# A planner's order in place of a scheduler's, in a kernel of linear attention and a feed-forward layer

## The chip, the cores and the metric

The kernel runs on one core of one Trainium2 chip. The metric is the device time of one execution in microseconds; the median of several executions counts, and lower is better.

## What is computed

The reference has two parts. The first is an attention without softmax that carries a state: for each of 4 batches and 8 heads, over 768 steps, with vectors of 48 numbers,

```
y[t]  = r[t] (state + (u * k[t]) v[t]^T)
state = w * state + k[t] v[t]^T
```

where `w` is a decay per head and channel (0.85 to 0.95 in the inputs) and `u` a bonus. The results of all heads form x, 3072 tokens of 384 numbers. The second part is a feed-forward layer:

```
h = x @ w_in          # 384 -> 2048
g = h - tanh(h)
out = g @ w_out       # 2048 -> 384
```

`r`, `k`, `v`, `w`, `u` come as float32. The two weights come as float64 (6.29 MB each); the kernel reads their 64-bit words as integers and makes float32 of them on the chip.

## The kernel before

**Units.** The attention part is cut into 24 units. A unit is 64 steps (`SHORT`) of two batches, all 8 heads. Unit n belongs to chunk n // 2, and the two units of a chunk cover the four batches. The function `near` is for decays near one (0.5 to 2); a flag, computed on the chip, says whether they are, and the function `anywhere` takes over if not. In this profile `near` alone does work.

**The steps of a unit** (`unit`, lines 385 to 470). Six DMAs of 96 KB bring r, k and v in two halves each. TensorE transposes r (`turn`, L402) into `x_ps`; VectorE multiplies it by the powers of the decay (`rT`, L411). k is multiplied by the inverse powers (`kw`, L413), transposed and copied by ACT (`kT`, L415). A product r*k*u, summed per head, gives `du` (L409, L417, L418), which becomes a diagonal `at` (L420, eight ACT instructions). TensorE multiplies the state by rT (L431), then kT by rT (the levels, L435). VectorE writes the levels into `at` where a mask says so (L437, the mask step). TensorE forms the outputs from v and `at` (L442) and the state's addition from kw and v (L449). ACT copies the outputs to `xt` and `rest` (L451, L456); after every second unit, POOL issues six small DMAs that fill the rest of `xt` (L460, the fills). VectorE adds to the state (L466), POOL multiplies it by the decay (L469). The first 16 units are "early": their r*k, u and kw products run on VectorE; in the later ones these and the diagonal run on POOL.

**Tiles.** Two units make a block of 256 tokens; there are 12. The 2048 hidden features are done 256 at a time; one block and 256 features is a tile, so there are 96. A tile has an h part (L156, 6 matmuls of 256 columns, in two halves, into one of two PSUM buffers), five ACT operations (L167 to L171: s, th, tg, q, small), four VectorE operations (L172 to L175: g, two products on tg, and a copy where x is small), and an o part (L184, 4 matmuls of 384 columns). Every matmul in float32 is two instructions in the profile. The o part of a tile is put two tiles behind its h part (the list `waiting`).

**Weights.** There are 16 pieces of 768 KB (`Weights`): two of w_in, two of w_out, in turn. A piece of w_in comes in four DMAs, one of w_out in one. Four staging buffers hold pieces. Converting a piece takes five VectorE and two ACT instructions (L130 to L140). In the kernel before, all pieces are loaded by POOL's queue, the next one into a buffer when its conversion is written out.

**What sets the order.** The first six blocks (`FIRST`) go through the features in four quarters: quarter 0 of blocks 0 to 5, then quarter 1, and so on, so that only a quarter of the weights is needed at first. Partial sums are kept (`part`) and added (L192). Blocks 6 to 11 take all features at once. Beside the tiles of blocks 0 to 5, the functions `weave` and `steady` mix the units of the blocks ahead and the conversions in proportion to their numbers of steps. The start up to unit 1 and pieces 0 and 1 is written out by hand (`go`), through the class `Written`, which keeps the order as written; its line in the profile is L230 for all operations. Behind that, the framework's own scheduler orders each engine's instructions from its own costs.

Of the kernel before, what the change touches and what calls it, by code (L numbers as in the profile page):

```python
# [2 lines left out]

# [6 lines left out]
F32 = mybir.dt.float32  # L10
U32 = mybir.dt.uint32
I32 = mybir.dt.int32
# [65 lines left out]
class Weights:  # L78
# [28 lines left out]
    def load(self, n, queue=None):  # L107
        if n >= self.count:
            return
        dst, parts = self.piece(n)  # L110
        if self.sources[n % 4 > 1].dtype == I64:
            self.staged[n] = st = self.stage.tile([128, self.COLS], I64, name="st", tag="st", bufs=4)
            dst = st.rearrange("p (k f) -> p k f", k=dst.shape[1])
        for to, src in parts:
            (queue or self.nc.sync).dma_start(out=dst[to], in_=src)  # L115

    def convert(self, n, V=None, A=None):


        if n not in self.staged:  # L120
            return
        V, A = V or self.nc.vector, A or self.nc.scalar
        dst = self.piece(n)[0].rearrange("p k f -> p (k f)")
        st = self.staged.pop(n)
        words = st.bitcast(U32).rearrange("p (n t) -> p n t", t=2)
        lo, hi = words[:, :, 0], words[:, :, 1]
        lo_f = st.bitcast(F32).rearrange("p (n t) -> p n t", t=2)[:, :, 0]
        power = self.stage.tile([128, self.COLS], U32, name="power", tag="power", bufs=2)
        bits = dst.bitcast(U32)
        V.tensor_scalar(power, hi, 0x7FF00000, None, ALU.bitwise_and)  # L130
        V.tensor_scalar(bits, hi, 0xFFFFF, 0x100000, ALU.bitwise_and, ALU.bitwise_or)
        yield
        A.activation(power, power, AF.Relu, scale=8.0, bias=self.bias)
        A.activation(lo_f, lo, AF.Copy, scale=2.0**-52)
        yield
        V.scalar_tensor_tensor(dst, bits, 2.0**-20, lo_f, ALU.mult, ALU.add)
        yield
        V.scalar_tensor_tensor(power, hi, 0x80000000, power, ALU.bitwise_and, ALU.bitwise_or)  # L138
        yield
        V.tensor_tensor(dst, dst, power.bitcast(F32), ALU.mult)  # L140
        yield


def make_dense(nc, work, gpool, ps_d, shared, out, rows):

    V, A, T = nc.vector, nc.scalar, nc.tensor
    d, w_in_sb, w_out_sb = (shared[x] for x in ("dims", "w_in", "w_out"))
    m1b, smallb = (shared[x] for x in ("m1b", "smallb"))

    waiting, sums = [], {}  # L150

    def first(xt, f):
        h = ps_d.tile([128, 2, d.NT], F32, name="h", tag="h")
        for z in range(2):
            for kk in range(d.NK):
                T.matmul(h[:, z], w_in_sb[:, f // 2, kk, z * 128 : (z + 1) * 128],  # L156
                         xt[:, kk].rearrange("p b t -> p (b t)"),
                         start=kk == 0, stop=kk == d.NK - 1)
        hf = h.rearrange("p z t -> p (z t)")

        def tmp(name):
            return work.tile([128, 2 * d.NT], F32, name=name, tag=name)

        s, th, tg, q, small = (tmp(x) for x in ("s", "th", "tg", "q", "small"))
        g = gpool.tile([128, 2, d.NT], F32, name="g", tag="g")
        gf = g.rearrange("p z t -> p (z t)")
        A.activation(s, hf, AF.Square)  # L167
        A.activation(th, hf, AF.Tanh)  # L168
        A.activation(tg, hf, AF.Tanh, scale=G1)  # L169
        A.activation(q, s, AF.Square, bias=m1b)  # L170
        A.activation(small, s, AF.Relu, bias=smallb, scale=-1.0)  # L171
        V.tensor_tensor(gf, hf, th, ALU.subtract)  # L172
        V.scalar_tensor_tensor(tg, s, C4, tg, ALU.mult, ALU.mult)  # L173
        V.scalar_tensor_tensor(tg, q, K1, tg, ALU.add, ALU.mult)  # L174
        V.copy_predicated(gf, small.bitcast(I32), tg)  # L175
        return g

    def second(j, fs, f, g):
        if f == fs[0]:
            sums["now"] = [ps_d.tile([128, d.DM], F32, name=f"o{i}", tag=f"o{i}", bufs=1) for i in range(L)]  # L180
        outs = sums["now"]
        for z in range(2):
            for i in range(L):
                T.matmul(outs[i], g[:, z, i * C : (i + 1) * C], w_out_sb[:, f + z, :],  # L184
                         start=f + z == fs[0], stop=f + z == fs[1] - 1)
        if f + 2 < fs[1]:
            return
        begun, whole = fs[0] > 0, fs[1] == d.NF
        for i in range(L):
            if begun:  # L190
                o = sums.pop((j, i)) if whole else sums[j, i]
                V.tensor_tensor(o, outs[i], o, ALU.add)  # L192
            else:
                if whole:
                    o = work.tile([128, d.DM], F32, name="o", tag="o")
                else:
                    o = sums[j, i] = work.tile([128, d.DM], F32, name="part", tag="part", bufs=L * FIRST)
                A.copy(o, outs[i])  # L198
            if whole:
                runs = rows(L * j + i)  # L200
                n = C // len(runs)
                for z, row in enumerate(runs):
                    nc.sync.dma_start(out=out[row : row + n, :], in_=o[z * n : (z + 1) * n])

    def dense(j, xt, fs=(0, d.NF)):

        for f in range(fs[0], fs[1], 2):
            waiting.append((j, fs, f, first(xt, f)))
            if len(waiting) > 2:
                second(*waiting.pop(0))  # L210
            yield

    def finish():
        while waiting:
            second(*waiting.pop(0))

    return dense, finish


class Written:  # L220


    def __init__(self, tc, engine):
        self.tc, self.engine, self.last = tc, engine, None

    def __getattr__(self, name):
        op = getattr(self.engine, name)

        def issue(*args, **how):
            self.last = self.tc.keep_in_program_order(op(*args, **how))  # L230
            return self.last

        return issue


def steady(d, first, unit, dense, finish, nstep, new_xt, xts):
# [5 lines left out]
    for j in range(0 if first else 2):  # L242
        weave(blocks(j))
    for j in range(first, d.NB):
        streams = [(dense(j, xts.pop(j)), d.NF // 2)]
# [7 lines left out]
def near(ctx, tc, r, k, v, w, u, out, shared, weights):  # L253
# [3 lines left out]
    V, A, T, G = nc.vector, nc.scalar, nc.tensor, nc.gpsimd  # L257
# [13 lines left out]

    engines = {x: Written(tc, getattr(nc, x)) for x in ("vector", "scalar", "tensor", "sync")}
    V, A, T, Q = engines.values()
    A.activation(fixed("warm", [128, 1]), shared["one"], AF.Tanh)
    ps = ps_a.tile([128, 2, 512], F32, name="x_ps", tag="x_ps")
    rows = fixed("rows", [NP, 2, PAD])
    V.memset(rows, 1.0)  # L280
    Q.dma_start(out=rows[:, :, :D], in_=w.rearrange("(p i) d -> p i d", i=2))
# [6 lines left out]
    ub = fixed("ub", [128, H, D])  # L288
# [10 lines left out]
    HALF = [slice(z * SHORT, (z + 1) * SHORT) for z in range(2)]  # L299
    loaded = {}  # L300

    def fetch(n, parts="rkv", queue=None):
        ch, half = divmod(n, 2)
        at = slice(ch * SHORT, (ch + 1) * SHORT)
        if n not in loaded:
            kt = load.tile([128, H, D], F32, name="kt", tag="kt")
            loaded[n] = {"r": rts[n % (AHEAD + 1)], "k": kt, "v": vts[n % (AHEAD + 1)]}
        for x in parts:
            src = {"r": r, "k": k, "v": v}[x]
            for z in range(2):  # L310
                (queue or Q).dma_start(out=loaded[n][x][HALF[z], :, :D],
                                       in_=src[half * 2 + z, :, at, :].rearrange("h t d -> t h d"))

    fetch(0, "r")
    fetch(0, "k", A)
    weights.load(0, G)
    Q.dma_start(out=ub.rearrange("p h d -> p (h d)"),
                in_=bass.AP(tensor=u.tensor, offset=u.offset, ap=[[0, 128], [1, H * D]]))
    fetch(1, "rk")
    weights.load(1, G)  # L320
    fetch(0, "v")
    fetch(1, "v")
    weights.load(2, G)
    weights.load(3, G)
    fetch(2)

    wcol = ps[:, 1, :NP]
    T.transpose(wcol, rows.rearrange("p i d -> p (i d)"), ident[:NP, :NP])  # L330
    power = fixed("power", [128, NP, SHORT + 1])
    inverse = fixed("inverse", [128, NP, SHORT + 1])
    V.tensor_scalar(by[:, :, 1:], wcol[:, :, None].to_broadcast([128, NP, SHORT]), W_LOW, W_HIGH, ALU.max, ALU.min)
    flat = "d p n -> d (p n)"
    V.tensor_tensor_scan(power.rearrange(flat), by.rearrange(flat), plus.rearrange(flat), 0.0, ALU.mult, ALU.add)
    V.reciprocal(inverse, power)

# [474 lines left out]
```

## Time and profile before

| | us |
|---|---|
| Median of 3 executions (655.8 to 656.92) | 656.14 |
| The profiled execution | 655.85 |
| Its span in the profile | 654.1 |
| TensorE matmuls busy | 604.0 |
| VectorE busy | 419.2 |
| ScalarE busy | 365.2 |
| GpSimd busy | 134.7 |

The profile is one execution, with times counted from the start of its span; what lies around the span is 1.75 us. PE is TensorE, DVE VectorE, ACT ScalarE, POOL GpSimd, SP the engine that issues most DMAs. "L383" is line 383 of the kernel. "Idle before" is the time that an engine stood before an instruction, and the name after the arrow is what ended it. DMA share is the mean busy share of the core's 16 DMA engines.

### The profile page before, as it was taken

The page shows a single profiled execution, that of the slowest core. Times are in us where ns is not written, and L with a number is a line of the kernel's source. Part 1 is how long each engine was busy: PE and PEld are TensorE (multiplying, and loading weights), DVE is VectorE, ACT ScalarE, POOL GpSimd, SP SyncE. Part 2 cuts the span into 40 slices and gives each one's busy share as a digit, 9 for nine tenths or more (in the row PEclk, how much of TensorE's full clock was granted, in tenths as well). Part 3 has the DMA queues.
Part 4 walks back from the last instruction along what each step waited for, and adds up shares of the span by engine and source line. Part 5 has one row for each costly group of instructions (what it writes and reads, how often), then busy time and mean ns, then how long its engine had stood idle before and what let it go on. Part 6 is the DMA issues. An engine that isn't in the chain of part 4 may idle for free.

```text
span 654.1 us, 12775 instructions
## 1 busy us (share of the span) xinstructions
PE 604.0 (92%) x5063; PEld 445.8 (68%) x5063; DVE 419.2 (64%) x659; ACT 365.2 (56%) x740; POOL 134.7 (21%) x185
## 2 busy tenths in 40 slices
PE   2358998999999999999999999999999999999994
PEld 1346765676777777777777777777777777777772
DVE  4578998999856566656665755646645544555551
ACT  3356876877665554555555554554554554655552
POOL 5142452546001121104000132332321201000000
PEclk9999999999999999999999999999999999999998
DMA  9897674871010100101011120220110000100001
GB/s 153 196 158 177 105 134 135 138 172 37 8 25 13 27 18 6 33 1 31 25 25 48 43 56 13 42 51 9 33 29 2 15 17 5 29 1 2 24 1 29
DMA packets 85857, 33.76 MB, mean 52 GB/s; under 512 B 78620, under 2 KB 82972, under 8 KB 85788
## 3 DMA queue, kind: packets, MB, share of 16 engines
q1 hardware_dynamic: 78972, 18.89, 15.9%
q0 software_dynamic: 5760, 13.77, 8.8%
q8 instruction: 42, 0.69, 0.4%
q10 hardware_dynamic: 1056, 0.20, 0.2%
q14 instruction: 27, 0.22, 0.1%
HBM read 26.94 MB, written 4.72 MB: 48 GB/s over the span
## 4 chain that ended last, share of the span: by engine, by line
PE 79%; DVE 8%; DMA 5%; issue 3%; ACT 2%; POOL 1%; SPq 1%; DVEq 0%; POOLq 0%
PE h L156 36%; PE o L184 35%; PE yk_ps L383 5%; DMA kt<-in_k_dram 2%; PE x_ps L402 2%; DMA st<-in_moe_w_out_dram 2%; PE x_ps L383 1%; DMA rt<-in_r_dram 1%; POOL xt L460 1%; SPq L230 1%; DVE g L172 1%; DVE power L138 1%; DVE at L437 0%; DVE tg L173 0%; DVE du L418 0%
## 5 line engine op out<-in xcount | busy, mean ns | idle before, releaser
L156 PE MATMUL h<-xt,w_in_sb 128*128 128x256 f32 x1152 | 273.0, 385 | 7.9 <-DMA xt<-rest 7.9
L184 PE MATMUL o<-w_out_sb,g 128*128 128x384 f32 x768 | 266.6, 488 | 3.1 <-ACT part L198 3.1
L156 PEld LDWEIGHTS h<-xt,w_in_sb 128*128 128x128 f32 x1152 | 214.0, 191 | 46.0 <-issue 7.7
L184 PEld LDWEIGHTS o<-w_out_sb,g 128*128 128x128 f32 x768 | 145.0, 190 | 83.5 <-ACT part L198 4.7
L172 DVE TENSOR_TENSOR g<-h,th 128x512 f32<-128x512 f32 x96 | 66.3, 690 | 188.3 <-ACT tg L169 188.3
L167 ACT ACTIVATE s<-h 128x512 f32<-128x512 f32 x96 | 57.3, 597 | 209.1 <-PE h L156 209.1
L175 DVE COPY_PREDICATED g<-small,tg 128x512 f32<-128x512 int32 x96 | 76.6, 797 | 6.0
L174 DVE SCALAR_TENSOR_TENSOR tg<-q,tg 128x512 f32<-128x512 f32 x96 | 67.5, 703 | 6.0
L170 ACT ACTIVATE q<-s,m1b 128x512 f32<-128x512 f32 x96 | 70.4, 733 | 0.0
L171 ACT ACTIVATE small<-s,smallb 128x512 f32<-128x512 f32 x96 | 70.1, 730 | 0.0
L173 DVE SCALAR_TENSOR_TENSOR tg<-s,tg 128x512 f32<-128x512 f32 x96 | 70.1, 730 | 0.0
L169 ACT ACTIVATE tg<-h 128x512 f32<-128x512 f32 x96 | 57.9, 603 | 0.0
L460 POOL DMA_DIRECT2D xt<-rest x72 | 37.4, 527 | 95.2 <-ACT rest L456 88.2
L168 ACT ACTIVATE th<-h 128x512 f32<-128x512 f32 x96 | 56.8, 592 | 0.0
L469 POOL TENSOR_TENSOR state<-state,power 128x384 f32<-128x384 f32 x22 | 32.2, 1465 | 56.1 <-DVE state L466 53.1
L422 POOL TENSOR_TENSOR at<-same,du 128x512 f32<-128x512 f32 x8 | 10.5, 1313 | 127.1 <-PE yk_ps L383 127.1
L420 ACT ACTIVATE at<-same,du 128x64 f32<-128x64 f32 x112 | 30.0, 342 | 11.9 <-PE yk_ps L383 7.7
L383 PEld LDWEIGHTS yk_ps<-rT,state 48*64 48x64 f32 x704 | 23.4, 140 | 9.3 <-issue 9.3
L409 POOL TENSOR_TENSOR rk<-rt,kt 128x384 f32<-128x384 f32 x8 | 8.2, 1020 | 103.3 <-DMA rt<-in_r_dram 100.3
L383 PE MATMUL yk_ps<-rT,state 48*64 48x64 f32 x704 | 26.4, 227 | 0.0
L115 POOL DMA_DIRECT2D st<-in_moe_w_in_dram x32 | 18.5, 582 | 31.8 <-ACT at L230 20.1
L383 PEld LDWEIGHTS yk_ps<-at,vt 64*64 64x64 f32 x768 | 14.4, 143 | 15.5 <-DVE at L437 5.8
(95 smaller groups left out, 424.5 us busy)
## 6 DMA issues: line engine op xcount, KB each, us to landing
st<-in_moe_w_out_dram POOLq DMA_DIRECT2D x8, 768.0 KB, 6.4
rt<-in_r_dram SPq DMA_DIRECT2D x48, 96.0 KB, 2.9
st<-in_moe_w_in_dram POOLq DMA_DIRECT2D x16, 288.0 KB, 5.5
vt<-in_v_dram SPq DMA_DIRECT2D x48, 96.0 KB, 3.0
kt<-in_k_dram SPq DMA_DIRECT2D x46, 96.0 KB, 3.4
out_dram<-part SPq DMA_DIRECT2D x24, 96.0 KB, 2.2
out_dram<-o SPq DMA_DIRECT2D x24, 96.0 KB, 2.2
st<-in_moe_w_in_dram POOLq DMA_DIRECT2D x16, 96.0 KB, 5.4
```

Source lines behind the costliest of these rows:

```text
L156: T.matmul(h[:, z], w_in_sb[:, f // 2, kk, z * 128 : (z + 1) * 128], xt[:, kk].rearrange("p b t -> p (b t)"), start=kk == 0, stop=kk == d. ...
L167: A.activation(s, hf, AF.Square)
L168: A.activation(th, hf, AF.Tanh)
L169: A.activation(tg, hf, AF.Tanh, scale=G1)
L170: A.activation(q, s, AF.Square, bias=m1b)
L171: A.activation(small, s, AF.Relu, bias=smallb, scale=-1.0)
L172: V.tensor_tensor(gf, hf, th, ALU.subtract)
L173: V.scalar_tensor_tensor(tg, s, C4, tg, ALU.mult, ALU.mult)
L174: V.scalar_tensor_tensor(tg, q, K1, tg, ALU.add, ALU.mult)
L175: V.copy_predicated(gf, small.bitcast(I32), tg)
L184: T.matmul(outs[i], g[:, z, i * C : (i + 1) * C], w_out_sb[:, f + z, :], start=f + z == fs[0], stop=f + z == fs[1] - 1)
L383: tc.keep_in_program_order(nc.tensor.matmul(*args, skip_group_check=True, **how))
```

## The change

The near-decay part is written as tasks for a planner. Each task has an engine, a cost in us, the tasks that it must follow, a due time, and for DMAs an amount of data. `Plan.order` first passes due times backward from each task to those before it, then runs through time: at each step, of the engines with a ready task, it takes the one that can start first, and on it the ready task with the earliest due time. A task of another engine is ready 0.16 us after its predecessor ends, of the same engine 0.06. DMAs share one channel of 230,000 bytes per us, with at most 8 under way per queue, and land 1.7 us after their issue at the earliest. r, k and v are entered with 175,000 bytes for each 98,304 moved. The instructions are then issued in the planned order, and every engine keeps it (`tc.manual_schedule()`); the scheduler has no part in it.

```
+class Plan:
+    HOP, NEAR_HOP, LANDS, RATE, LANES = 0.16, 0.06, 1.7, 230e3, 8
+    def add(self, engine, cost, run, after=(), due=1e9, data=0):
+        t = SimpleNamespace(engine=engine, cost=cost, run=run, after=[x for x in after if x], due=due, data=data,
+                            then=[], ready=0.0, n=len(self.tasks))
...
+    def order(self):
+        for t in reversed(self.tasks):
+            for x in t.then:
+                t.due = min(t.due, x.due - t.cost - self.HOP - (self.LANDS if t.data else 0))
...
+        while any(waiting.values()):
+            best = None
+            for e, ts in waiting.items():
+                if ts:
+                    start = max(free.get(e, 0.0), min(x.ready for x in ts))
+                    t = min((x for x in ts if x.ready <= start + 1e-9), key=lambda x: (x.due, x.n))
+                    if t.data:
+                        start = max(start, lanes.setdefault(e, [0.0] * self.LANES)[0])
+                    if best is None or start < best[0]:
+                        best = start, t
...
-    fetch(0, "r")
-    fetch(0, "k", A)
-    weights.load(0, G)
...
+    for n in range(weights.count):
+        queue, name = (Q, "SP") if n < 4 else (G, "POOL")
+        step = steps(lambda n=n, queue=queue: weights.load(n, queue))
+        free = converted[n - 4] if n >= 4 else None
...
+        exp = add("DVE", .47, step, of + ([converted[n - 2]] if n >= 2 else []))
+        power2 = add("ACT", .84, step, [exp])
+        low = add("ACT", .84, step, [power2])
+        mant = add("DVE", .47, step, [low])
+        now = add("DVE", .87, step, [mant])
...
+        x.turn = add("PE", .5, lambda: turn(rt), [x.r, b1.cp, tabs, downs, flagged])
+        x.rT = add("DVE", .62, scale_r, [x.turn, ups])
+        x.kw = add(e, cost, lambda: E.tensor_tensor(kw[:, :, :D], t.kt, w_down, ALU.mult), [x.k, downs, b2.out])
+        turn_k = add("PE", .5, lambda: turn(kw), [x.kw, x.rT])
+        x.kT = add("ACT", .5, copy_k, [turn_k])
...
+        x.lev = add("PE", .56, levels, [x.kT, x.rT, now])
+        x.cp = add("DVE", .64, lambda: V.copy_predicated(t.at, before, lev), [x.lev, x.diag])
+        x.out = add("PE", 1.05, outputs, [x.cp, x.v, b1.xt, b1.rest, b1.add])
...
+        now = add("PE", 1.29, lambda: dense.h(t, 0), filled[j, "all"] + [converted[piece], b1.h, b2.s, b2.th, b2.tg, b2.g], due)
+        x.h = add("PE", 1.29, lambda: dense.h(t, 1), [now], due + 1.3)
...
+        now = add("PE", 1.3, lambda: dense.o(t, 0), [x.cp, converted[piece + 2], b1.o] + b1.empty, due + 2 * pace)
+        x.o = add("PE", 1.3, lambda: dense.o(t, 1), [now], due + 2 * pace + 1.3)
...
+    now, part = 26.0, d.NF // 4
+    for q in range(4):
+        for j in range(FIRST):
+            for f in range(q * part, (q + 1) * part, 2):
+                pace = 5.2 + (3.7 if q == 0 and j < FIRST - 1 else 1.25 if q < 3 else 0)
+                hidden(j, (q * part, (q + 1) * part), f, now, pace)
+                now += pace
...
+    for j in range(FIRST, d.NB):
+        for f in range(0, d.NF, 2):
+            hidden(j, (0, d.NF), f, now, 6.0)
+            now += 5.2 + (.95 if j + 2 < d.NB else 0)
+    for t in plan.order():
+        t.run()
```

Only tiles have due times of their own; units, conversions and loads get theirs from the tiles that need them. The same instructions are there on the compute engines, with these differences: the conversion's second VectorE step comes after the two ACT steps; a tile's h and o parts are halves that can be placed apart; the early units' eight diagonal instructions are two groups of four; the flag is computed before the first r is transposed, where it was finished at the end of quarter 0. Of the DMAs, weight pieces 0 to 3 go through SP's queue and not POOL's, and unit 0's k through SP's and not ACT's. The function `make_dense` becomes the class `Dense`, whose order `anywhere` writes out.

## The prediction

> **What bounds the kernel now.** I read the busy times first, then busy time by stage, then the timelines of TensorE, VectorE and POOL around the stage borders. The page:
>
> ```profile
> PE 604.0 (92%) x5063; PEld 445.8 (68%) x5063; DVE 419.2 (64%) x659; ACT 365.2 (56%) x740; POOL 134.7 (21%) x185
> ```
>
> The average hides two regimes. Busy time by stage, stages cut at events of the timelines (columns: stretch, length, then busy us of PE, PEld, DVE, ACT, POOL, granted clock, DMA share, GB/s):
>
> ```profile
> 0.00:44.50 44.50, 14.56 (x223) 11.09 (x223) 23.74 (x46) 15.56 (x34) 17.84 (x45) 1.00 0.90 171
> 58.30:147.30 89.00, 78.99 (x1313) 57.56 (x1312) 85.08 (x144) 69.39 (x168) 38.59 (x52) 0.98 0.69 145
> 147.30:155.70 8.40, 6.79 (x22) 4.12 (x23) 8.40 (x14) 5.01 (x14) 5.90 (x7) 1.00 0.29 61
> 155.70:645.60 489.90, 489.90 (x3285) 361.89 (x3283) 288.70 (x437) 265.15 (x498) 69.46 (x79) 1.00 0.10 21
> ```
>
> To 44.5 us the DMA engines are 90% busy and VectorE half idle; from 58.3 to 147.3 VectorE is 96% busy; from 155.7 TensorE never stops. So the end is fixed by how much TensorE work is done before 155.7. VectorE's early idle time and unit 11, the last that the first quarter of the hidden features needs:
>
> ```profile
> 22.47 0.56 DVE L230 TENSOR_TENSOR rk<-rt,kt 128x384 f32<-128x384 f32 x1 [9.39 <-DMA kt<-in_k_dram]
> 58.26 0.71 DVE L437 COPY_PREDICATED at<-before,x_ps 128x512 f32<-128x512 int32 x1
> 145.38 0.72 DVE L437 COPY_PREDICATED at<-before,x_ps 128x512 f32<-128x512 int32 x1
> ```
>
> The first is VectorE standing 9.39 us for unit 1's k; the others are the masks of units 3 and 11. TensorE after unit 11's mask:
>
> ```profile
> 146.66 0.63 PE L383 MATMUL yk_ps<-vt,kw 64*64 64x48 f32 x32
> 147.67 4.14 PE L184 MATMUL o<-w_out_sb,g 128*128 128x384 f32 x12 [0.38 <-ACT part L198]
> 152.43 1.10 PE L156 MATMUL h<-xt,w_in_sb 128*128 128x256 f32 x4 [0.62 <-DMA xt<-rest]
> 155.73 3.62 PE L156 MATMUL h<-xt,w_in_sb 128*128 128x256 f32 x16
> ```
>
> Unit 11's matmuls end at 147.3, and the fills of its xt reach h 5.1 us later. The tail:
>
> ```profile
> 637.70 7.90 PE L184 MATMUL o<-w_out_sb,g 128*128 128x384 f32 x24
> 645.64 0.48 ACT L198 COPY o<-o 128x384 f32<-128x384 f32 x1 [0.17 <-PE o L184]
> ```
>
> TensorE ends at 645.6, 8.5 us before the span's end.
>
> **A check of the account.** The chain of waits gives 2.59 us for a tile's h and 2.58 for its o: 5.17 a tile; four tiles with one unit take 24.57 us (374.78 to 399.35), so a unit costs TensorE 24.57 - 4 x 5.17 = 3.89. At the end of unit 11, 10 tiles of h and 8 of o stand before it in the built program. Left: 96 x 5.17 - 10 x 2.59 - 8 x 2.58 = 449.8, and 12 units, 46.7, less 1.0 for two without state updates: 495.5. 147.3 + 495.5 = 642.8; measured 645.6, so 2.8 us of stalls.
>
> **What the Trainium skill says.** "DMA: Bandwidth & Descriptors", section "Issuing engines are not separate DMA queues": transfers issued by SP, ACT and POOL run on the same 16 DMA engines. The trace agrees: 0.90 share with three issuers at work, so moving loads between queues buys order, not bandwidth. "GPSIMD Engine Reference", section "1. Specifications": its SBUF interfaces are shared with VectorE. The trace agrees; one operation, with VectorE partly idle and with it full:
>
> ```profile
> 33.79 0.84 POOL L469 TENSOR_TENSOR state<-state,power 128x384 f32<-128x384 f32 x1 [0.51 <-DVE state L230]
> 153.82 5.80 POOL L469 TENSOR_TENSOR state<-state,power 128x384 f32<-128x384 f32 x1
> ```
>
> "TensorE: Matmul & The Clock Gate", section "What's actually happening": an idle array runs at half clock. Four transposes take 1.12 us at 33.26 and 0.60 at 53.02.
>
> **The change part by part.** No arithmetic is added: 80 conversion instructions, 16 early units and 96 tiles on VectorE in both. What moves is order.
>
> *Loads.* Weight pieces 0 to 3 (10 DMAs) go from POOL to SP, and unit 0's k (2 DMAs) from ACT to SP. Up to piece 3, SP has 30 DMAs, 30 x 0.65 = 19.5 us of issuing from 1.2; bytes arrive more slowly, so this is covered. Without POOL's eight early weight DMAs beside them, unit 1's r and k come ahead of the weights. Issued by 8.7 at 0.65 each, they land by 12.1 (3.4 us, the row of kt), against 22.5.
>
> *Start.* VectorE has rk, kw and rT of unit 0 done by 14.7 (the flag, now ahead of the first r transposes, costs a wait to 12.7, named here since everything queues behind it); k transposes 1.1, kT 0.7, levels 1.1, mask 0.7 and hand-overs bring unit 0's mask to 18.8 (before 27.7). Unit 1, whose r transposes wait for that mask: r 1.1, rT 0.7, unit 0's outputs beside it, k 1.1, kT 0.7, levels 1.1, mask 0.7 and some 0.2 per hand-over, 6.5 us with a cold array: 25.3 (before 33.2). Unit 2, as long, some 33.6. Unit 3 needs 4 x 0.59 MB of r, k, v, four pieces of 0.79 and u of 0.2, 5.7 MB: at 171 GB/s 33.4 us, plus 2.1 to the first issue and 3 to land, 38.5. Its kw, transposes, kT, levels and mask add 5 to 6: 44.5 (before 58.9). Bounds 41 and 49: pieces 4 and 5 (POOL) may share the engines or not.
>
> *Units 4 to 11.* VectorE instructions between the masks of units 3 and 11 in the built order, priced start to start: 58 of 0.47 (rk, kw, du, state, first two of a conversion), 35 of 0.60 (rT, g, tg), 8 masks of 0.62, 8 copies of 0.63, 21 conversions of 0.87: 27.3 + 21.0 + 5.0 + 5.0 + 18.3 = 76.6. Before: 81.8 by the same count, in 87.1 measured, a ratio of 1.06. After: 81.4. TensorE has 8 units and 9.5 h and 8 o halves, 76.3 us (before 71.6), so two engines are nearly full; I add 2. Unit 11's mask ends at 44.5 + 81.4 + 2 = 127.9, its matmuls at 129.2, against 147.3: **18 us earlier with the same tiles done**. Bounds 119 (41, no idle) and 140.
>
> *After unit 11.* 24 conversions remain, against 17 before. VectorE work from that mask to the end of tile 19's copy is 52.9 us, TensorE's 54 us: no reserve. By cumulated work each o follows its copy by 1 to 2 us, and the h of tile 13 waits 1.2 us for tile 11's g (13.4 against 12.5, plus hand-over). The fills of unit 11 are covered by two units' transposes and 2 tiles of o (7.3 us for 5.1 to 8). I take 4 us of stalls, bounds 1 and 10.
>
> *Blocks 8 to 11.* The planner runs tiles until none is left, then fits in the missing units: unit 16 ends at tile 63.5 and unit 18 at 64.5, where before they stood at 51 and 59. From unit 17's last matmul to the first h of block 8 there are three half-o groups (1.29), r and k (0.44 each), and state and levels (1.55): 6.3 us; needed are copies 0.75, six fills 2.9 and landing 2.2, 5.9. Hidden just so; 1 us for each of four blocks: 4, bounds 0 and 10.
>
> *At nothing.* Halves h and o alternate (3 and 2 matmuls instead of 6 and 4): the weight loads run beside the matmuls in both; if not, the tile pitch would show it. ACT's split diagonals: ACT is 78% busy in the unit stage. The tail: the same last o, copy and stores, 8.5.
>
> Sum: 129.2 + 495.5 + 4 + 4 + 8.5 = 641.2 span. The profiled execution took 655.85 for 654.1, so +1.75: 642.95; the median shown, 656.14, lies 0.3 above it: **643**.
>
> **The rivals.** (1) *Less gain.* By the copy of tile 19 VectorE's cumulated work is 162.7 us in both orders, and before it had idled 28 us at unit 11's mask. If it idles as long in the new order, unit 11 ends at 109.8 + 28 + 1.3 = 139.1 and the total is 653. For it: a fixed order can't fill a late wait with a conversion. Against: most of the 28 us lie before 49 us and come from late k. (2) *More gain.* VectorE full from 41: 118.9 + 495.5 + 3 + 8.5 + 2 = 628. (3) *Slower, by late units.* If in blocks 8 to 11 the cover fails, because POOL's operations or a copy on ACT stand behind others, each block pays the path from mask to h: 1.1 + 0.75 + 2.9 to 4.0 + 2.2 = 7 to 8 us. Four times 8 in place of the 4 counted: 671. It decides from 4.3 us a block on, which eats the 13 us. For it: before, these units ended some 9 tiles before the tile that needs them, now none, and POOL's work in them is 1.0 to 1.5 us a piece. Against: VectorE is 59% and POOL 14% busy there. (4) That the order is not kept: the built list shows it as planned.
>
> **How the numbers follow.** About 0.2% (1.3 us) is what a measurement can tell. The forecast, 635 to 649, has 0.50; more gain 0.17; less gain, to 655, 0.17; slower 0.16. Range 628 to 658. Faster 0.80, same 0.05, slower 0.15.
>
> **What would show it.** Right: unit 1's k landed by 13; mask of unit 3 near 44 and of unit 11 near 128; TensorE without gaps over 2 us after 140; tile pitch 5.17. Wrong: unit 11's mask after 140; waits of h on the fills of xt of several us near tiles 64, 72, 80 and 88; POOL's state products of over 3 us ahead of a state matmul.

## The result: no change, and the profile after

The changed kernel took 656.76 us (median of 4 executions, 655.46 to 657.02), the kernel before 656.22 beside it (4 executions, 655.8 to 656.92): a ratio of the means of 1.0003 with a 95% interval of 0.9986 to 1.0020. The forecast was 643. The profiled execution took 655.46 for a span of 653.7.

The busy times of the profile after, by engine:

```profile
PE 609.2 (93%) x5063; PEld 447.9 (69%) x5063; DVE 427.0 (65%) x659; ACT 366.7 (56%) x740; POOL 117.5 (18%) x175
```

The numbers of instructions are the same (POOL's ten fewer, 175 for 185, are the ten weight DMAs that SP issues now), but TensorE's busy time rose by 5.2 us (604.0 before) and VectorE's by 7.8 (419.2): single instructions became longer. Busy time by stage, at the same four cuts as before:

```profile
0.00:44.50 44.50, 21.39 (x373) 17.21 (x375) 30.41 (x56) 18.92 (x45) 13.98 (x36) 1.00 0.90 168
58.30:147.30 89.00, 80.94 (x1240) 59.40 (x1241) 84.48 (x134) 69.18 (x165) 31.42 (x51) 1.00 0.66 129
147.30:155.70 8.40, 7.63 (x60) 5.95 (x59) 8.40 (x14) 7.13 (x13) 2.04 (x2) 1.00 0.32 96
155.70:645.60 489.90, 486.25 (x3215) 354.90 (x3214) 291.57 (x438) 263.17 (x496) 63.99 (x78) 1.00 0.10 21
```

To 44.5 us VectorE is busy 6.7 us longer than before at the same DMA share (0.90): the start did become fuller. In the last stretch TensorE, which had never stopped before, has 3.65 us without work. Three VectorE instructions, the product r*k of unit 1 and the masks of units 3 and 11:

```profile
11.61 0.56 DVE L486 TENSOR_TENSOR rk<-rt,kt 128x384 f32<-128x384 f32 x1 [1.55 <-DMA kt<-in_k_dram]
...
49.25 0.72 DVE L563 COPY_PREDICATED at<-before,x_ps 128x512 f32<-128x512 int32 x1
...
137.77 0.73 DVE L563 COPY_PREDICATED at<-before,x_ps 128x512 f32<-128x512 int32 x1
```

k of unit 1 is there at 11.6, where VectorE had stood until 22.5. But the lead shrinks: 9.0 us at unit 3's mask, 7.6 at unit 11's. TensorE around the end of unit 11, and at the tail:

```profile
139.07 0.63 PE L436 MATMUL yk_ps<-vt,kw 64*64 64x48 f32 x32
...
145.78 5.34 PE L160 MATMUL h<-xt,w_in_sb 128*128 128x256 f32 x24
151.89 1.56 PE L160 MATMUL h<-xt,w_in_sb 128*128 128x256 f32 x6 [0.77 <-DVE g L184]
153.38 1.15 PE L436 MATMUL yk_ps<-rT,state 48*64 48x64 f32 x32
```

```profile
642.89 2.85 PE L196 MATMUL o<-w_out_sb,g 128*128 128x384 f32 x8 [0.26 <-DVE g L190]
645.77 0.48 ACT L210 COPY o<-o 128x384 f32<-128x384 f32 x1 [0.17 <-PE o L196]
```

Unit 11's matmuls end at 139.7 (147.3 before) with as many tiles done, and the last o ends at 645.7 (645.6 before). So the whole account has two lines: **the stage up to unit 11 became 7.6 us shorter, and the stage after it 7.7 us longer** (506.0 us from unit 11's matmuls to the last o, against 498.3). These two numbers, "start" and "rest", are given for every experiment below. The two rests by busy time (columns as above), first before, then after the change:

```profile
147.30:645.60 498.30, 496.69 (x3306) 366.01 (x3306) 297.10 (x450) 270.16 (x512) 75.36 (x85) 1.00 0.10 22
```

```profile
139.70:645.70 506.00, 501.59 (x3305) 366.04 (x3304) 307.57 (x463) 275.95 (x518) 69.89 (x86) 1.00 0.11 24
```

TensorE is busy 501.6 us in place of 496.7, and without work 4.4 in place of 1.6: of the 7.7 us, 4.9 are longer work for the same instructions and 2.8 are waits.

### The profile page after: what moved, and what is told of

Read it like the earlier page. It is cut to its first block, busy times and chain, and to the rows that moved or that the text cites. A ratio compares the mean times of both kernels' runs of the same rounds, so it can differ in the third digit from the quotient of the medians.

```text
span 653.7 us, 12709 instructions
## 1 busy us (share of the span) xinstructions
PE 609.2 (93%) x5063; PEld 447.9 (69%) x5063; DVE 427.0 (65%) x659; ACT 366.7 (56%) x740; POOL 117.5 (18%) x175
## 4 chain that ended last, share of the span: by engine, by line
PE 79%; DVE 11%; ACT 3%; issue 2%; DMA 2%; SPq 1%; DVEq 0%; POOL 0%; ACTq 0%; POOLq 0%
PE h L160 34%; PE o L196 34%; PE yk_ps L436 6%; PE x_ps L474 2%; PE x_ps L436 2%; DVE g L190 1%; DMA vt<-in_v_dram 1%; DVE tg L188 1%; SPq L462 1%; DVE tg L186 1%; DMA st<-in_moe_w_in_dram 1%; DVE g L184 1%; DVE at L563 1%; DVE rT L478 1%; DVE w_out_sb L135 1%
## 5 line engine op out<-in xcount | busy, mean ns | idle before, releaser
L196 PE MATMUL o<-w_out_sb,g 128*128 128x384 f32 x768 | 281.7, 492 | 5.1 <-DVE g L190 5.1
L160 PE MATMUL h<-xt,w_in_sb 128*128 128x256 f32 x1152 | 281.9, 382 | 0.8 <-DVE g L184 0.8
L196 PEld LDWEIGHTS o<-w_out_sb,g 128*128 128x128 f32 x768 | 141.3, 190 | 69.9 <-DVE g L190 8.2
L188 DVE SCALAR_TENSOR_TENSOR tg<-q,tg 128x512 f32<-128x512 f32 x96 | 73.2, 762 | 6.6
L190 DVE COPY_PREDICATED g<-small,tg 128x512 f32<-128x512 int32 x96 | 72.5, 756 | 6.6
L553 POOL TENSOR_TENSOR kw<-kt,w_down 128x384 f32<-128x384 f32 x8 | 8.4, 1045 | 223.5 <-PE yk_ps L436 223.3
L568 POOL TENSOR_TENSOR state<-state,power 128x384 f32<-128x384 f32 x22 | 25.2, 1144 | 82.7 <-DVE state L546 63.0
L497 ACT ACTIVATE at<-same,du 128x64 f32<-128x64 f32 x128 | 33.2, 344 | 11.4 <-DVE du L490 11.4
L531 ACT COPY xt<-yk_ps 128x384 f32<-128x384 f32 x24 | 11.5, 478 | 33.7 <-PE yk_ps L436 25.1
L563 DVE COPY_PREDICATED at<-before,x_ps 128x512 f32<-128x512 int32 x24 | 17.4, 726 | 16.8 <-PE x_ps L436 13.8
```

What stands on the lines that cost most here:

```text
L160: self.nc.tensor.matmul(t.h2[:, z], self.w_in_sb[:, t.f // 2, kk, z * 128 : (z + 1) * 128], self.xts[t.j][:, kk].rearrange("p b t -> p (b ...
L188: V.scalar_tensor_tensor(t.tg, t.q, K1, t.tg, ALU.add, ALU.mult)
L190: V.copy_predicated(t.g, t.small.bitcast(I32), t.tg)
L196: self.nc.tensor.matmul(self.outs[i], t.g2[:, z, i * C : (i + 1) * C], self.w_out_sb[:, t.f + z, :], start=t.first and z == 0, stop=t.last ...
```

## The experiments

Theories after this comparison. *Loads*: what shortened the start is the new order of the loads on SP alone. *Collisions*: the start stayed 10.5 us behind the forecast because VectorE's instructions are slowed by POOL's product of the state with the decay beside them. *Borders*: the rest is longer because small and large matmuls of a unit and a tile meet more often. *Cover*: it is longer because tiles cut in halves leave less time between a tile's h and its o. *Late units*: the units of the last blocks come in bunches at the last moment. The rival to all of these is that issuing as written costs, since no engine can step past a late operand.

Each number of start and rest is from one profiled execution. Five of them with the same instructions up to unit 11 (the changed kernel, join, early, join_early, gluelate) have starts of 139.7 to 141.1, so a difference in start of under 1.4 us says nothing. The rest repeats better: after, nodecay and poolq, with one order behind unit 11, have 506.0 to 506.1. The times are medians of 4 to 22 executions; the ratios are to executions of the kernel before on the same chip, and so not the quotients of the medians shown. The profiled execution can be one of the fastest (655.46 after the change, 658.06 in join). In brackets behind the rest stand TensorE's busy time in it and its time without work.

| kernel | start | rest (busy + without work) | median us | ratio to before (95%) |
|---|---|---|---|---|
| before | 147.3 | 498.3 (496.7 + 1.6) | 656.2 | 1 |
| after | 139.7 | 506.0 (501.6 + 4.4) | 656.8 | 1.0003 (0.9986 to 1.0020) |
| join | 140.3 | 508.1 (499.2 + 8.9) | 661.8 | 1.0087 (1.0065 to 1.0109) |
| early | 140.3 | 506.1 (501.4 + 4.7) | 657.4 | 1.0014 (1.0002 to 1.0026) |
| join_early | 140.2 | 503.4 (497.5 + 5.8) | 655.0 | 0.9981 (0.9971 to 0.9990) |
| glue | 142.6 | 503.4 (499.7 + 3.7) | 656.5 | 0.9998 (0.9983 to 1.0013) |
| gje | 143.6 | 503.5 (497.8 + 5.7) | 657.3 | 0.9998 (0.9983 to 1.0014) |
| gluelate | 141.1 | 503.4 (499.7 + 3.7) | 655.5 | 0.9983 (0.9968 to 0.9998) |
| nodecay | 136.3 | 506.0 (501.6 + 4.4) | 652.2 | 0.9940 (0.9919 to 0.9962) |
| nodecay_je | 136.9 | 502.2 (497.3 + 4.9) | 649.8 | 0.9887 (0.9868 to 0.9905) |
| poolq | 148.6 | 506.1 (501.6 + 4.5) | 666.1 | 1.0149 (1.0127 to 1.0171) |
| sched | 150.7 | 511.5 (504.4 + 7.1) | 672.6 | 1.0247 (1.0221 to 1.0273) |
| loads | 142.7 | 499.8 (498.4 + 1.4) | 652.3 | 0.9930 (0.9905 to 0.9955) |
| loads_u0 | 138.2 | 500.6 (498.4 + 2.2) | 649.2 | 0.9898 (0.9858 to 0.9937) |

### Borders: join

The state matmuls of units 12 to 21 are put next to the level matmuls, as they stood before the change.

```
+        if n >= 12 and now:
+            joined.append((now, x.lev))
...
-    for t in plan.order():
+    order = plan.order()
+    for state_step, level_step in joined:
+        order.remove(state_step)
+        order.insert(order.index(level_step), state_step)
+    for t in order:
         t.run()
```

> In the planner's order the 16 state matmuls of a unit and its 16 level matmuls stand apart, with tiles between; the scheduler's order had them side by side. In the trace the pair took 1.64 us of TensorE side by side and 1.18 + 0.83 = 2.01 apart. This kernel keeps the planned order but moves the state matmuls of units 12 to 21 to directly before the level matmuls. Theory (borders between small and large matmuls cost TensorE time, and give back part of the early gain): ten units by 0.37, so 3.7 us less than the planned kernel, about 653, and V to V of units 12 and 13 goes from 56.0 to 55.6. Rival (the loss is in waits of the late units alone): no change, or longer, since the levels come later by 0.9 us.

What a border costs is read from the starts of the large groups around it, half a tile's h or o being 1.29 us. TensorE in the kernel before, with a whole o (8 instructions), state and levels together, and h:

```profile
419.64 2.74 PE L184 MATMUL o<-w_out_sb,g 128*128 128x384 f32 x8
...
423.29 0.64 PE L383 MATMUL x_ps<-rT,kT 48*64 48x64 f32 x30
423.86 2.86 PE L156 MATMUL h<-xt,w_in_sb 128*128 128x256 f32 x12
426.56 2.74 PE L184 MATMUL o<-w_out_sb,g 128*128 128x384 f32 x8
```

426.56 - 419.64 is 6.92; less two groups of 2.58 this is 1.76 us for state and levels. In the changed kernel they stand apart:

```profile
207.95 1.46 PE L160 MATMUL h<-xt,w_in_sb 128*128 128x256 f32 x6
209.33 1.15 PE L436 MATMUL yk_ps<-rT,state 48*64 48x64 f32 x32
210.41 1.56 PE L196 MATMUL o<-w_out_sb,g 128*128 128x384 f32 x4
211.81 1.46 PE L160 MATMUL h<-xt,w_in_sb 128*128 128x256 f32 x6
...
219.56 1.46 PE L160 MATMUL h<-xt,w_in_sb 128*128 128x256 f32 x6
220.95 0.69 PE L436 MATMUL x_ps<-rT,kT 48*64 48x64 f32 x32
221.57 1.56 PE L196 MATMUL o<-w_out_sb,g 128*128 128x384 f32 x4
222.97 1.46 PE L160 MATMUL h<-xt,w_in_sb 128*128 128x256 f32 x6
```

The state matmuls take 211.81 - 207.95 - 2 x 1.29 = 1.28 us and the levels 222.97 - 219.56 - 2.58 = 0.83, together 2.11 or 0.35 more. No wait is shown at either place; the group after the small matmuls is itself longer (1.56 for 1.45). In join the distance from unit 12 to unit 13 went from 55.95 to 55.65, about as the border theory says, and TensorE's busy time in the rest fell by 2.4 us. Yet join is slower than before by 0.9%, where 653 us was expected, and its rest is 2.1 us longer: 4.5 us more are without work. The waits of TensorE after 140 us in join (us in total, times, the longest):

```profile
PE o L196 <- DVE g L190: 7.0, 8, 1.6
```

After the change they are 2.7 us. The state matmuls stand later in join, so a unit's mask may come late in the bunches of the last blocks, and with it the tiles' copies on VectorE; that is argued from the waits, not shown. Nor does this profile show all of it: the profiled execution was the fastest of eight, 3.7 us below the median. The border itself is real and worth 0.3 to 0.35 us a unit.

### Late units: early and join_early

Units 16 to 23 get due times of their own, one unit per four tiles; join_early is this and join together.

```
-        x.out = add("PE", 1.05, outputs, [x.cp, x.v, b1.xt, b1.rest, b1.add])
+        x.out = add("PE", 1.05, outputs, [x.cp, x.v, b1.xt, b1.rest, b1.add],
+                    331.9 + 8 * 6.15 * (j - FIRST) - (50, 25)[slot] if j >= FIRST + 2 else 1e9)
```

> Units 16 to 23 get due times of their own, 50 and 25 us ahead of the first tile that needs them, so that the planner spreads them one per four tiles and does not fit two in at the last moment. Theory (the last-minute units drain the tiles in flight, and h and o then wait for VectorE: 2.8 us more of stalls after unit 11 than before, all near tiles 64, 72, 80 and 88): 3 us less than the planned kernel, and the idle times of PE before o at 449, 501, 552, 600 and 610 us go. Rival (they are covered): within 1 us of the planned kernel.

> Both: state matmuls next to the levels for units 12 to 21, and due times of their own for units 16 to 23. Theory: the two gains add, 6 to 7 us less than the planned kernel, about 650, so about 6 us (0.9%) less than the kernel before. That is most of the 7.7 us by which unit 11 ends earlier. Rival (the early gain is lost in something common to both kernels, such as a TensorE rate): no more than 2 us below the kernel before.

In early the units are spread: their last matmuls, from unit 16 on, end at 392.6, 417.8, 444.5, 469.8, 495.8 and 520.7. That is 25.6 us for four tiles and a unit, where the kernel before takes 24.57, and the time did not move: spreading alone gained nothing. Together the two edits gain: the rest falls from 506.0 to 503.4, and the time is 0.19% under that of before, though 655.0 and not the expected 650. TensorE's busy time falls by 4.1 us, of the 4.9 that the change had added, and 1.4 us more are without work. The waits of TensorE after 140 us, first after the change, then in join_early:

```profile
PE o L196 <- DVE g L190: 2.7, 6, 0.7
...
PE h L160 <- DVE g L184: 0.8, 1, 0.8
```

```profile
PE o L196 <- DVE g L190: 3.3, 3, 1.3
PE yk_ps L436 <- DVE at L565: 1.6, 3, 0.6
PE h L160 <- DVE g L184: 0.8, 1, 0.8
```

o still waits for VectorE's last copy into g in three places.

### Cover: glue, gje and gluelate

In glue the first half of each tile's o is moved down to its second half, so that tiles are whole on TensorE; gluelate does this from tile 8 on only; gje is glue with join and early.

```
+        pairs.append((now, x.o))          # gluelate: if m >= 8
...
+    order = plan.order()
+    for first, second in pairs:
+        order.remove(first)
+        order.insert(order.index(second), first)
+    for t in order:
         t.run()
```

> As after the change, but once the planner has ordered everything, the first half of each tile's o is moved down to directly before its second half: h and o of a tile are whole again on TensorE, nothing else moves. Theory, the halves cost slack: with halves alternating, 6 groups of 1.29 us lie between a tile's last h and its first o (7.75 us); with whole tiles it is 8 (10.3 us). The chain from h over ACT and VectorE to the copy of g is what o waits for, so 2.6 us more cover should take the waits of o on g after 140 us from 2.7 us (6 of them) to under 1, and the time from 656.7 to about 654.5. Rival, the stalls come from VectorE being late by more than that or from h waiting for g: waits of 2 us or more remain, and the time stays within 1.3 of 656.7. Tile pitch 5.17 in both.

> Three edits together on the changed kernel: whole tiles of o as in glue, the state matmuls moved next to the level matmuls for units 12 to 21, and due times of their own for units 16 to 23, one unit per four tiles. Theory: the late part of the changed kernel loses 4.8 us at unit borders and 5.6 in stalls; with the units spread, the waits of o on g (3.3 us in join_early, 1.3 the longest) fall under 1.5 thanks to 2.6 us more cover, so 655.0 becomes 652.5 to 653.5, below the kernel before (656.7) by 0.5 to 0.6%. Rival, the cover does not matter: 654.5 to 655.5, as join_early.

> As glue, but only for tiles 8 and later; the tiles up to unit 11 keep their halves as after the change. Theory, glue gained and lost in two places: after unit 11 it took 503.3 us of TensorE in place of 505.9 (no wait of o on g left), and up to unit 11 it lost 2.9 (142.6 against 139.7), since an o put off by half a tile puts off what VectorE gets. With the early half left alone: unit 11's matmuls end within 0.7 of 139.7, waits of o on g after 140 under 0.5 us, time 654.1 (653.3 to 655), ratio 0.996. Rival, the 2.6 us come from where tiles and units meet by chance and not from the cover: 656 to 657.

The waits of TensorE after 140 us in glue:

```profile
PE x_ps L474 <- DVE rT L478: 1.9, 3, 0.9
PE yk_ps L436 <- DVE at L563: 1.8, 2, 0.9
PE h L160 <- DVE g L184: 0.8, 1, 0.8
```

No o waits for g any longer, and the rest is 2.7 us shorter. But the cover is only a part of that. Other waits have grown: transposes wait 1.9 us for rT (0.9 before this edit) and a unit's matmuls 0.9 for a mask (the other half of the 1.8 is unit 11's own wait, which belongs to the start). TensorE's time without work in the rest falls by 0.8 us alone, from 4.42 to 3.67. The other 1.9 us are busy time (501.6 to 499.7). With whole tiles fewer stretches of a unit's small matmuls stand between large groups in the rest (32 for 35 in the traces), so these are probably borders again, which is close to the rival named for gluelate. No run separates the two.

glue's start is 2.9 us longer, so its time is the same: up to unit 11, where VectorE is full, half a tile of o put off may be work that comes later. gluelate leaves the early half alone and keeps the shorter rest (503.4) with the same waits. Its start of 141.1 lies within the spread of equal starts, and its median is 1.3 us below that of the changed kernel, not the expected 2.6; as the intervals of the two ratios overlap, a gain in time isn't shown. In gje the outputs wait for masks instead (4.9 us, 7 times), and it is no faster than before, where 652.5 to 653.5 was expected; the three edits do not add up.

### Collisions: nodecay and nodecay_je

For units 0 to 11 the product of the state with the decay on POOL is left out (that state is then not decayed); nodecay_je does it in join_early.

```
-        x.decay = add("POOL", .9, lambda: G.tensor_tensor(state[:, :, :, :D], ...
+        x.decay = add("POOL", .9, lambda: n >= 12 and G.tensor_tensor(state[:, :, :, :D], ...
```

> The planned kernel with the same order of everything else, but POOL's product of the state with the decay left out for units 0 to 11. Theory (between the masks of units 3 and 11 VectorE instructions that overlap a POOL state product run 0.3 to 1.5 us longer, 4.7 us in sum, against 1.3 in the kernel before; and three before unit 3's mask, 2 us): unit 11's mask ends 5 to 7 us before 138.5, at 132 to 134, and the total is 4 to 7 us less. Rival (VectorE's fixed order waits for something else in those places): the long instructions go but waits take their place, and unit 11's mask moves by less than 2 us.

> join_early with POOL's product of the state with the decay left out for units 0 to 11 (that state is then not decayed), same order. Theory, what is gained in the VectorE-bound start and what is gained in the TensorE-bound rest add up, since TensorE never has a long gap after unit 11: nodecay took 4.5 us off and join_early 1.7, so 650.4 (649.5 to 651.5), with unit 11's mask at 135 and the last copy of g at 636.5. Rival, the rest is bound by VectorE in places and eats an earlier start: 652 or more, waits of o on g over 6 us.

One conversion step on VectorE (at 41.20), with its neighbours, and POOL's product beside it, in the changed kernel:

```profile
39.86 0.56 DVE L546 TENSOR_TENSOR state<-yk_ps,state 128x384 f32<-128x384 f32 x1 [1.42 <-ACT xt L531]
40.34 0.95 DVE L133 SCALAR_TENSOR_TENSOR w_out_sb<-w_out_sb,st 128x768 f32<-128x768 uint32 x1
41.20 1.60 DVE L134 SCALAR_TENSOR_TENSOR power<-st,power 128x768 uint32<-128x768 uint32 x1
42.72 0.68 DVE L478 TENSOR_TENSOR rT<-x_ps,w_up 128x512 f32<-128x512 f32 x1
```

```profile
40.50 1.49 POOL L568 TENSOR_TENSOR state<-state,power 128x384 f32<-128x384 f32 x1 [2.48 <-DVE state L546]
```

and the same step in nodecay:

```profile
41.53 0.95 DVE L134 SCALAR_TENSOR_TENSOR power<-st,power 128x768 uint32<-128x768 uint32 x1
```

The collision is real: 0.65 us for this step. In the changed kernel ten VectorE instructions up to unit 11 are longer by 0.4 to 1.1 us than others of their kind, each beside such a product; before there were four, and in nodecay there is none. "GPSIMD Engine Reference", section "1. Specifications", of the Trainium skill says that GpSimd's SBUF interfaces are shared with VectorE; the trace agrees, and 0.65 us is what it costs in this place. The whole worth is less than the sum, though: unit 11's mask came 3.4 us earlier and not 5 to 7 (the time, 4.6 us below the changed kernel's, is in the expected 4 to 7), since VectorE then waits more elsewhere (at 40.19 in nodecay 3.59 us for ACT's copy of xt, where it had waited 1.42). That a shorter chain from unit to unit gave the 3.4 us is unlikely: up to 140 us no matmul of the changed kernel waits last for that product. nodecay_je met its expectation (649.8 for 650.4): a gain in the start and a gain in the rest add, because TensorE is the limit in the rest (busy 497.3 of its 502.2 us).

### Loads: poolq, loads and loads_u0

poolq is the changed kernel with weight pieces 0 to 3 issued by POOL again.

```
-        step = steps(lambda n=n, queue=queue: weights.load(n, queue))
+        step = steps(lambda n=n: weights.load(n, G))
```

> The order of all instructions as after the change, but the ten DMAs of weight pieces 0 to 3 are issued by POOL again instead of SP (the planner still plans them as SP's, so their place in the order stays). Theory, the queue is what brings the first units forward: POOL's DMAs again run beside SP's r and k, so k of unit 1 lands after 16 us (11.6 after the change, 22.5 before it), unit 1's mask ends at 30 to 33 (26.3 after, 33.2 before), unit 11's 2 to 4 us later than 138.5, and the time is 659 to 661. Rival, the order alone does it: k of unit 1 by 13, unit 1's mask within 1 us of 26.3, unit 11's within 1.5 of 138.5, time within 1.3 of the changed kernel's 656.7.

VectorE's products r*k of units 0 and 1 in poolq:

```profile
12.12 0.56 DVE L486 TENSOR_TENSOR rk<-rt,kt 128x384 f32<-128x384 f32 x1 [5.40 <-DMA kt<-in_k_dram]
...
21.09 0.56 DVE L486 TENSOR_TENSOR rk<-rt,kt 128x384 f32<-128x384 f32 x1 [5.27 <-DMA kt<-in_k_dram]
```

Both k are late again; unit 0's mask ends at 27.7 as before the change (18.6 after it), unit 1's at 35.4, unit 11's at 147.4 (138.5). The direction is the expected one and the size is larger: unit 11's mask was to be 2 to 4 us later and the time 659 to 661. Of the 9.2 us at unit 0, 8.9 are still there at unit 11 and 9.0 at the last o. With the old queue the planner's order has a start of 148.6, the old order 147.3. **With the ten weight DMAs back in POOL's queue nothing of what the change gained is left**, though unit 0's k still goes through SP. (The kind of queue changes with the order: the profile calls POOL's software_dynamic and SP's hardware_dynamic. No run separates the two, but to 44.5 us about as many bytes moved either way, 171 GB/s before and 168 after.) The opposite test follows: the kernel before, its own scheduler and order, with this one part of the change.

```
-    fetch(0, "r")
-    fetch(0, "k", A)
-    weights.load(0, G)
+    fetch(0, "rk")
     Q.dma_start(out=ub ...
-    fetch(1, "rk")
-    weights.load(1, G)
     fetch(0, "v")
+    fetch(1, "rk")
+    weights.load(0, Q)
     fetch(1, "v")
-    weights.load(2, G)
-    weights.load(3, G)
+    weights.load(1, Q)
     fetch(2)
+    weights.load(2, Q)
+    weights.load(3, Q)
```

> The kernel before, with its own orders on every engine and its scheduler, and one edit: unit 0's k and weight pieces 0 to 3 are issued by SP, in the order in which the changed kernel's SP issues them. Theory, the load queue is the whole of what the change gains, and the written order gives it back: poolq showed the queue worth 9 us at unit 0's mask, carried unchanged to the end; the kernel before spends 498.3 us of TensorE after unit 11, the changed one 505.9. So unit 0's mask ends at about 19 (27.7 before the change), unit 1's at 26 (33.2), unit 11's at 138 (146.1), and the time is 648 (646 to 651), a ratio of 0.987. Rival, the old order of VectorE and TensorE cannot use earlier r and k, since conversions written ahead of unit 1 now wait for weight pieces that land later: unit 3's mask stays above 55, unit 11's above 143, time 653 or more.

It is faster than both kernels by 0.7%, but 4 us short of the theory, and unit 0's mask ends at 22.6 in place of 19. VectorE in loads shows where:

```profile
17.81 0.56 DVE L230 TENSOR_SCALAR power<-st 128x768 uint32<-128x768 uint32 x1 [4.36 <-DMA st<-in_moe_w_in_dram]
...
21.86 0.73 DVE L230 COPY_PREDICATED at<-before,x_ps 128x512 f32<-128x512 int32 x1 [1.96 <-ACT kT L230]
```

The hand-written start puts the first conversion ahead of unit 0's mask, and its weights now come later than r and k. So one more edit:

```
-    go(units, 0, 0, 0, 0, 1, 0)
-    go(pieces, 0)
-    go(units, 1, 1, 0)
-    go(pieces, 0)
+    go(units, 0, 0, 0, 0, 1, 0, 0)
+    go(units, 1, 1)
+    go(pieces, 0, 0)
```

> As loads, and unit 0's mask and unit 1's rT and kw are written ahead of the first two conversion instructions on VectorE, which in loads stood 4.4 us for weight piece 0 (17.8) with unit 0's mask behind them (22.6). Theory, loads fell 4 us short of its 648 because of that wait alone: unit 0's mask ends at 16.5 to 17.5, unit 1's at 24, unit 11's at 137 to 138.5 (140.6 in loads), time 649 to 650, ratio about 0.989. Rival, VectorE's own work binds from about 40 us on and the start of unit 0 does not carry: unit 11's mask within 1 us of 140.6, time 651.5 to 653.

```profile
15.68 0.72 DVE L230 COPY_PREDICATED at<-before,x_ps 128x512 f32<-128x512 int32 x1 [2.51 <-PE x_ps L382]
16.30 0.68 DVE L230 TENSOR_TENSOR rT<-x_ps,w_up 128x512 f32<-128x512 f32 x1
```

The mask of unit 0 stands 6.2 us earlier, unit 11's ends at 136.8 for 140.6, and the time is 649.19: **1.0% faster than before, the best that was run with all of the work in it**. Its start is 138.2 and its rest 500.6. The 2.3 us of rest over the 498.3 of the kernel before are mostly work that moved: at the end of unit 11, 7.25 tiles of o are done in place of 8, and 0.75 x 2.58 is 1.9. With these counted, its start is level with the planner's (140.2 against 139.7 to 141.1) and its rest with that of the kernel before (498.6). The masks came within 0.2 us of the expected times, that of unit 1 1.4 us late, and the time is the expected one.

### As written: sched

The planner's list is given to the framework's scheduler as the program, and not kept as written.

```
-        with tc.manual_schedule():
-            near(tc, r, k, v, w, u, out, shared, weights)
+        near(tc, r, k, v, w, u, out, shared, weights)
```

> The planner's list is handed to the language's scheduler as the program's order, instead of being issued as written; loads and planner unchanged. Theory, that engines issue as written costs nothing by itself; it is the places of the units in the list that cost (TensorE's order of units among tiles from tile 16 on is the same in the built program): unit 1's mask within 1.5 us of 26.3, the late unit cost again 4.3 us (56.0 from unit 12's to unit 13's matmuls), time 655 to 659. Rival, the fixed order is what gives the gain back, since VectorE cannot step past a late operand: unit 11's mask at 134 or earlier, fewer stalls after it, time 652 or less.

Neither expected time was met; the run is 16 us slower than the changed kernel. VectorE in sched:

```profile
40.63 0.69 DVE L186 SCALAR_TENSOR_TENSOR tg<-s,tg 128x512 f32<-128x512 f32 x1 [6.63 <-ACT tg L173]
...
48.87 0.74 DVE L563 COPY_PREDICATED at<-before,x_ps 128x512 f32<-128x512 int32 x1 [2.17 <-PE h L160]
```

The scheduler puts a tile's products ahead of unit 2, VectorE stands for them, and unit 2's mask ends at 49.6 where it had ended at 36.6. So this does not say what a freer order would have given; it says that for this list the scheduler's own times serve worse. That a fixed order costs in general stays open. What the runs exclude is that it is needed for the gain: the two kernels that the scheduler ordered from the old program, loads and loads_u0, are the faster ones.

## Why the prediction was wrong

Two terms failed. One is the way of VectorE to unit 11's mask, which took 138.5 us for a predicted 127.9. The other is TensorE's work after unit 11, taken over from the kernel before as 495.5 us, where TensorE was busy 501.6. By the prediction's own steps, against a sum of 641.2 for the span (653.7 measured):

- **Loads: right.** k of unit 1 landed by 11.6 (12.1 predicted), unit 0's mask ended at 18.6 (18.8), unit 1's at 26.3 (25.3). poolq shows that the queue of the loads is the cause.
- **Unit 2 and unit 3: 3.0 and 5.5 us late.** Their masks ended at 36.6 and 50.0 (33.6 and 44.5 predicted). I had priced unit 3 from the landing of its data. Its r was transposed by 40.25, but rT of unit 3 starts at 42.72: on VectorE's fixed order it stands behind the state's addition, which waits 1.42 us for ACT's copy of xt, and two conversion steps, one of them in a collision. kw follows at 44.66, behind another conversion.
- **Units 4 to 11: 5.1 us late, the ratio of 1.06.** The 76.6 us of VectorE's base work were counted about right. I multiplied them by 1.06, the ratio seen before, and added 2; measured were 88.5 in place of 83.4. In the trace idle time is 6.2 us (3.9 before), instructions longer beside POOL's products 4.7 (1.3); with the 76.6 this leaves 1.0 of the 88.5 unexplained. A ratio taken from one order did not hold for the other, which places POOL's products beside VectorE's work. I had quoted the shared interfaces, and put no price on them; nodecay puts it at 3.4 us of the start.
- So unit 11's matmuls ended at 139.7 and not 129.2. The *less gain* rival said 139.1. That was luck: it let VectorE idle as long as before, but up to that mask VectorE idled 20.3 us for 25.2, and longer instructions made up the difference. Its 653 also took the rest as the prediction had it.
- **The rest: 495.5 + 4 + 4 predicted, 506.0 measured.** The failed term is the 495.5. It took TensorE's work from the kernel before, a unit at 3.89 us; TensorE was busy 6.1 us longer than that (in the kernel before 1.2 us longer). In the changed kernel unit 12 to unit 13 with ten tiles takes 56.0, or 4.3 a unit; 0.3 to 0.35 of this is the state matmuls standing apart (join), and with them moved and the late units spread the busy time is 497.5 (join_early). The waits came to 4.4 us of the 8 allowed, 2.7 of them o waiting for g. Here the prediction put halves "at nothing": the tile pitch did stay at 5.17, and that was the wrong place to look. Six half groups of 1.29 between a tile's last h and its first o, 7.75 us, are less cover than four whole ones, 10.3. With the cover back (glue) the waits of o are gone, but others took most of their place.
- **The tail: right**, 8.0 us for 8.5. The median lies above the profiled execution by 1.3 us, where 0.3 was taken.
- **The slower rival** did not come: no h waits for the fills of xt in blocks 8 to 11, and spreading those units (early) changed nothing by itself.

In sum 10.5 us were lost in the start, 2.5 in the rest, and 0.5 gained in the tail: 12.5 of the span's 653.7 - 641.2. The expected gain of 18 us did exist at unit 11, with 7.6 of it, and the rest took these back.

## What to carry to other kernels

When one edit changes the order of loads and the order of everything else, take the loads by themselves first: here they were worth 1% with the start's order adjusted, and all the rest of the rewrite gained nothing at the start and cost 7.7 us later. Where an engine never stops, price a moved step with the borders that it makes, by the distance between the starts of the groups around it, not by its own duration. And cutting work in halves to alternate it leaves the pitch alone but shortens the time that other engines have between a producer and its consumer; watch that wait, and the sum of all waits with it, since here a wait that was taken away came back in other places.

## What was not expected of the hardware

- A group of large matmuls after small ones of 64 columns is 0.11 us longer (1.56 for 1.45 for half an o), with no wait shown; a second such border within a unit cost 0.35 us. A group after a wait is longer too (half an h at 151.89 took 1.56 for 1.46).
- When a VectorE step and POOL's product of 128x384 overlap, who loses differs: at 41.20 after the change a step of 0.95 us took 1.60 and the product 1.49; at 36.96 a step of 0.55 took 1.48 and the product, from 37.16, only 0.86. Both cases look like the two taking turns: at 41.20 the product (0.84 at its shortest) ends about as if it had waited for the step before, which ends at 41.29, and the step as if it had waited for the product, which ends at 41.99. This is an estimate from these two places.
- The granted clock fell in the start of some runs, without a harm that shows. The clock's line of early and of loads_u0, whose slices are 16 us each:

```profile
PEclk9758999999999999999999999999999999999998
```

```profile
PEclk9759899999999999999999999999999999999998
```

In early the clock was 0.5 in the slice from 33 to 49 us, and unit 11's matmuls ended at 140.3, as in join, which had no dip. loads_u0 had such a dip too and the best time of the runs with all of the work.
